# Sliding-window attention and a feed-forward layer on one core: part of the first batch's V is loaded in runs of five rows, TensorE puts the rows in order, and w_in is loaded after all of V

## The chip, the cores and the metric

The kernel runs on one core of one Trainium2 chip. A core has TensorE (PE, matrix products; weight loads into it are listed apart as PEld), VectorE (DVE), ScalarE (ACT), GpSimd (POOL) and SyncE (SP, which here only issues transfers), and 16 DMA engines that move data between the chip's memory and the core's SBUF. TensorE writes to PSUM; here DVE and ACT read PSUM. The metric is the device time of one execution in microseconds (us). Before the change it is 318.2 us, the median of three runs (317.32 to 319.56).

## The reference

```python
def _attn_ref(q, k, v):                 # (8, 8, 576, 64) each: batch, head, position, width
    scores = (1 / sqrt(D)) * q @ k.transpose(0, 1, 3, 2)
    mask = abs(pos[:, None] - pos[None, :]) <= 32
    scores = where(mask, scores, -1e9)
    attn = softmax(scores)
    return attn @ v

def _moe_ref(x, w_in, w_out, s, b):     # x: 4608 x 512, w_in: 512 x 2048, w_out: 2048 x 512
    r = maximum(x @ w_in, 0)
    return (s * r * r + b) @ w_out
```

The attention's heads are put side by side to make x. The input and output are float32; the kernel multiplies in bf16.

## The kernel before

All 8 batches go through in one stream. A batch has 576 positions, cut into 9 tiles of 64; two tiles make a **unit** of 128 keys, so batch 0 has units 0 to 3 and a last unit 4 of 64 keys. For batch 0 q and k are loaded in pairs of heads (`load_pair`, L583), cast to bf16 (L592, L593), turned by TensorE (L599), copied out of PSUM (L605, L606), multiplied to scores (L832) and put through exp (L854). V is loaded by unit (`load_v`, L566): 128 keys on the 128 partitions, and on each the 8 heads of that key, which lie far apart in memory, so that a row moved is 64 float32, 256 bytes. `cast_v` (L575) casts a unit to bf16 into the tile `vb`. For each unit TensorE multiplies the exponentials by `vb` (L747), where a column of ones in `vb` makes the softmax's sums; unit u needs V of units u and u-1. DVE takes the reciprocal of the sums (L769) and normalises (L771), TensorE turns the result (L778) and ACT copies it to `xt` (L786), the layer's input.

The feed-forward layer goes over blocks of positions: the first four blocks hold 96, 128, 128 and 160 positions. `s1` multiplies a block by w_in (L980), ACT takes the relu (L987) and DVE the square (L989) into `gt`; `s2` multiplies by w_out (L998). For the first four blocks `early` does it in small groups (L1029) as parts of w_out arrive. w_in comes in four quarters of two loads each (`load_weights`, L538), cast by POOL (L541); w_out likewise, into the same eight staging buffers `STG`, so a load of w_out waits until POOL has cast what was in its buffer.

The order of the work is not written by hand beyond the loads: every step is a task with an engine, a cost in ns, what it reads and writes, and a key. `_Graph.plan` goes through the tasks with these costs and fixes one order for each engine; `emit` adds the waits. On the chip each engine then does its tasks strictly in that order, so a task that waits holds all that stands behind it on its engine. The loads of the start have ordered keys (`nxt()`) and go out on one queue, SP's, in the order in which they are written: q and k in pairs, then `ORDER0`, then s and b, w_out, and the second batch's q, k and V.

Before the change `ORDER0` is units 0 and 1 of V, the first quarter of w_in (its number 8), units 2, 3 and 4 of V, and the other three quarters of w_in (9 to 11):

```python
ORDER0 = (0, 1, 8, 2, 3, 4, 9, 10, 11)
EV0 = ("pool", "dve", "pool", "dve", "pool")     # which engine casts each unit of V
```

Of the kernel before, what the change touches and what calls it, by code (L numbers as in the profile page):

```python
# [7 lines left out]
BF16 = mybir.dt.bfloat16  # L8
# [3 lines left out]
S = 576  # L12
D = 64
# [4 lines left out]
NPAIR = H // 2  # L18
NTILE = S // 64
NUNIT = (NTILE + 1) // 2  # L20
# [4 lines left out]
LAG = 1  # L25
K0 = ("dve", "dve", "dve", "dve")
Q0 = ("act", "pool", "pool", "pool")
ORDER0 = (0, 1, 8, 2, 3, 4, 9, 10, 11)
WINE = ("pool", "pool", "pool", "pool")
FIRST = ((0, 0), (1, 0), (2, 0), (0, 1), (1, 1), (2, 1), (3, 0), (3, 1), (0, 2), (1, 2), (2, 2), (3, 2), (0, 3), (1, 3), (2, 3), (3, 3))  # L30
WOUTE = (("pool", "pool"),) * 4
# [9 lines left out]
CASTE = (("pool", "pool"), ("pool", "dve"))  # L41
SLACK = (1000.0, 2000.0, 3000.0, 3000.0)
PACEV = ((-1,-1,0,0,1),(0,0,1,1,2),(0,0,1,1,2))
EV0 = ("pool", "dve", "pool", "dve", "pool")
BANK1 = ("W", "SC", "SC", "AVN", "AVN")
EV1 = ("pool", "pool", "pool", "pool", "pool")
EV2 = ("dve",) * 5
# [24 lines left out]
class _Graph:  # L72
# [13 lines left out]
    def add(self, stream, fns, cost, reads=(), writes=(), key=0.0, accum=False, dma=None, waits=(),  # L86
            lat=None, slack=0.0):
        if not isinstance(fns, list):
            fns = [fns]
        after = [self.chain] if key < -100 and self.chain else []  # L90
        t = _Task(len(self.tasks), stream, fns, cost, self.LAT[stream] if lat is None else lat, key,
                  dma, slack, after)
        t.deps.update(waits)
        for a in after:
            assert a.stream == stream
            a.next.append(t)
        for r in reads:
            assert r in self.writer, r
            t.deps.add(self.writer[r])
        for w in writes:  # L100
            if w in self.writer:
                t.deps.add(self.writer[w])
            if not accum:
                t.deps.update(self.readers.get(w, ()))
        t.deps.discard(t)
        for r in reads:
            self.readers.setdefault(r, []).append(t)
        for w in writes:
            self.writer[w] = t
            if not accum:  # L110
                self.readers[w] = []
        self.tasks.append(t)
        if key < -100:
            self.chain = t
        return t
# [201 lines left out]
def bass_sliding_window_symmetric__then__act_starrelu_kernel(  # L317
# [23 lines left out]
    with ExitStack() as es:  # L341
# [11 lines left out]
        def sb(shape, dt, nm):  # L353
            uid["n"] += 1
            return es.enter_context(nc.sbuf_tensor(f"{nm}_{uid['n']}", list(shape), dt))
# [31 lines left out]
        ONESW = sb((128, 128), BF16, "onesw")  # L387
        IDENT = sb((128, 128), BF16, "ident")
        GT = [sb((128, 16, 512), BF16, "gt") for _ in range(2)]
        R1 = [sb((128, 512), BF16, "r1") for _ in range(NR1)]  # L390
        OUTS = [sb((128, DM), F32, "outs") for _ in range(NOUT)]
        CVEC = sb((128, DM), F32, "cvec")
# [134 lines left out]
        def load_weights(which, i, x, key, eng):  # L527

            si = take("stg", NSTG)
            stg = STG[si].rearrange("p (a c) -> p a c", a=2)  # L530
            if which == "in":
                src = moe_w_in.rearrange("(kc p) f -> p kc f", p=128)[:, 2 * x:2 * x + 2, i * 512:(i + 1) * 512]
                dst = WIN_BF[:, 2 * x:2 * x + 2, i * 512:(i + 1) * 512]
            else:
                f0 = 4 * i + 2 * x
                src = moe_w_out.rearrange("(fc p) c -> p fc c", p=128)[:, f0:f0 + 2, :]
                dst = WOUT_BF[:, f0:f0 + 2, :]
            add("sp", lambda e: e.dma_start(stg, src), 600.0, writes=[("STG", si)], key=key,  # L538
                dma=("l", 16, 100.0 if which == "in" else 85.0))
            land[which, i, x] = g.tasks[-1]  # L540
            add(eng, (lambda e: e.copy(dst, stg)) if eng == "act" else (lambda e: e.tensor_copy(dst, stg)),  # L541
                {"act": 1040.0, "dve": 690.0, "pool": 1100.0}[eng], reads=[("STG", si)], writes=[("W" + which, i, x)],
                key=key + 150.0, slack=100.0)
# [12 lines left out]
        def load_v(c, u, key, eng, waits=()):  # L556

            vs = number(c, u) % NUNIT
            ts = tiles(c, u)
            at = [tile_at(c, t) for t in ts]  # L560
            if len(at) == 2 and at[0][0] == at[1][0]:
                at = [at[0] + (0, 128)]
            else:
                at = [x + (64 * i, 64) for i, x in enumerate(at)]
            n = sum(x[3] for x in at)
            add(eng, [lambda e, b=b, j=j, p0=p0, m=m: e.dma_start(  # L566
                VST[p0:p0 + m, vs, :, :], v[b, :, 64 * j:64 * j + m, :].rearrange("h p d -> p h d"))
                for b, j, p0, m in at],
                (650.0 if eng == "sp" else 500.0) * len(at), writes=[("VST", vs)], key=key, dma=("l", n // 2, (20.0, 17.0, 23.0)[min(c, 2)]), waits=waits)
            land["v", c, u] = g.tasks[-1]  # L570

        def cast_v(c, u, key, eng, slack):
            vs, vb, n = number(c, u) % NUNIT, number(c, u) % (2 * NUNIT), 64 * len(tiles(c, u))
            add(eng, (lambda e: e.copy(VB[0:n, vb, :, 0:D], VST[0:n, vs, :, :])) if eng == "act" else
                (lambda e: e.tensor_copy(VB[0:n, vb, :, 0:D], VST[0:n, vs, :, :])),  # L575
                {"act": 617.0, "dve": 420.0, "pool": 750.0}[eng],
                reads=[("VST", vs)], writes=[("V", vb)], key=key, slack=slack)

        def load_pair(b, name, pr, load_key):

# [310 lines left out]
        def attention():  # L891
            seq = {"k": -200.0}

            def nxt():
                seq["k"] += 1.0
                return seq["k"]

            def w(which, i):
                for x in (0, 1):
                    load_weights(which, i, x, nxt(), WINE[i] if which == "in" else WOUTE[i][x])  # L900

            for pr in range(NPAIR):
                for name in "qk":
                    load_pair(0, name, pr, nxt())
                    turn_pair(0, name, pr, -60.0 + 0.1 * pr, banks, K0[pr] if name == "k" else Q0[pr], 200.0)
                pair_scores(0, pr)
            for t in ORDER0:
                if t < 8:
                    load_v(0, t, nxt(), "sp")
                    cast_v(0, t, -28.0 + t, EV0[t], 300.0)  # L910
                else:
                    w("in", t - 8)
            first_units()
            masks(land["av", 0, NUNIT - 1])
            for i, src in enumerate((moe_s, moe_b)):
                add("sp", lambda e, i=i, src=src: e.dma_start(SROW[0:128:32, i:i + 1], src.partition_broadcast(4)),
                    600.0, writes=[("SROW", i)], dma=("l", 1, 15.0), key=nxt())
            add("dve", lambda e: e.stream_shuffle(SB128[:, :], SROW[:, :], [0] * 32), 150,
                reads=[("SROW", 0), ("SROW", 1)], writes=[("SB128", 0), ("SB128", 1)], key=P2[0] - 8.0, slack=500.0)
            for step in ORDER1:  # L920
                if step[0] == "w":
                    w("out", step[1])
                elif step[0] == "v":
                    load_v(1, step[1], nxt(), "sp")
                    cast_v(1, step[1], due(1, 0) - 4.0 + step[1], EV1[step[1]], 800.0)
                else:
                    for name in "qk":
                        load_pair(1, name, step[1], nxt())
            yield S
            for pr in range(NPAIR):  # L930
                for name in "qk":
                    turn_pair(1, name, pr, due(1, 0) - 4.0 + 0.1 * pr, banks, "dve" if name == "k" else "pool", 500.0)
                pair_scores(1, pr)
            for u in range(NUNIT):
                if u == NUNIT - 1:
                    pe_part(due(1, u) - 3.0, None, qk_part(1, u))
                    exp_mask(1, u, due(1, u) - 3.0)
                last.append((1, u))
                close()
                yield closed[0]  # L940
            for b in range(PAIRS, B):
                c = seq_of(b)
                later(b, due(c, group_of(b)[0]) - 24.0)
                for i, u in enumerate(group_of(b)):
                    load_v(c, u, due(c, u) - 35.0, late(b), [paced(b, PACEV[min(b, 4) - 2][i])])
                    cast_v(c, u, due(c, u) - 4.0, EV2[i], SLACK[3])
                for u in group_of(b):
                    unit(c, u)
                    yield closed[0]
            if seq_tiles(LONG) % 2 == 0:  # L950
                unit(LONG, seq_units(LONG) - 1)
            while last:
                close()
            yield T
# [373 lines left out]
```

## Time and profile before

| | |
|---|---|
| median of 3 runs | 318.2 us |
| the profiled execution | 316.0 us |
| its span, from the first instruction to the last | 314.2 us |
| busy in the span | PE 297.0, DVE 190.1, ACT 140.8, POOL 89.3 us |
| first matmul of attention times V (L747) | at 14.25 us |
| first matmul of the layer (L980) | at 17.33 us |
| casts of w_in by POOL | the first at 14.28 us, the last at 29.02 us |

Times in the profile count from the span's start. In a row of the timeline stand the start, the duration (of the whole run of like instructions), the engine, the line and operation, the tiles written and read, the tile or shape, the count, and in square brackets how long the engine had been idle and what released it. In the chain of waits, which is followed back from the last instruction, stand start, duration and what that time was; "issue" is time in which the engine waited for nothing that the profile shows. In the page's slices each digit is a fortieth of the span, in tenths. In a window's row stand the window, its length, the busy time of PE, PEld, DVE, ACT and POOL with the number of instructions, the clock granted to TensorE as a share of the full one, the mean busy share of the 16 DMA engines, and GB/s.

### The profile page before, as it was taken

What the parts mean: (1) busy time and instruction counts of PE and PEld (TensorE: products, weight loads), DVE (VectorE), ACT (ScalarE), POOL (GpSimd) and SP (SyncE); (2) the same over time, 40 slices, a digit from 0 to 9 for tenths busy, and PEclk for the clock granted to TensorE, in tenths of its full rate; (3) what the DMA queues carried; (4) which work ended last, traced back from release to release, by engine and by line L of the source; (5) the groups of instructions that cost most, each with busy time, mean ns of one, the idle gap of its engine ahead of it and who ended that gap; (6) DMA issues with size and microseconds to landing.
All of it is one profiled execution on the core that took longest, in us unless ns stands there. A gap on an engine that the chain in (4) does not pass through costs nothing.

```text
span 314.2 us, 8417 instructions
## 1 busy us (share of the span) xinstructions
PE 297.0 (95%) x3557; PEld 162.3 (52%) x3602; DVE 190.1 (61%) x377; ACT 140.8 (45%) x219; POOL 89.3 (28%) x109
## 2 busy tenths in 40 slices
PE   7698999899999999999999999999999999999995
PEld 3477855477644554544444444444444444444444
DVE  3455594875796796887578477856555543333312
ACT  4736435266635775653266335444444333333300
POOL 3468864635136136132313421260000000000000
PEclk9969999999999999999999999999999999999999
DMA  7999999998998998798999799997111110100122
GB/s 261 296 303 392 388 286 282 191 172 263 254 166 210 288 160 163 237 228 140 219 297 165 161 190 336 166 157 176 52 52 50 52 46 33 37 35 33 37 96 74
DMA packets 98985, 56.13 MB, mean 179 GB/s; under 512 B 74048, under 2 KB 88128, under 8 KB 98944
## 3 DMA queue, kind: packets, MB, share of 16 engines
q1 hardware_dynamic: 98944, 55.56, 74.8%
q8 instruction: 29, 0.48, 0.7%
q14 instruction: 12, 0.10, 0.1%
HBM read 36.70 MB, written 9.44 MB: 147 GB/s over the span
## 4 chain that ended last, share of the span: by engine, by line
PE 79%; DMA 9%; DVE 4%; issue 3%; POOL 2%; ACT 2%; SPq 1%; POOLq 0%
PE w L980 34%; PE o L998 32%; DMA stg<-in_k_dram 4%; PE avn L747 3%; DMA stg<-in_moe_w_in_dram 3%; DMA vst<-in_v_dram 2%; PE o L1029 2%; PE avn L1029 2%; DVE gt L989 2%; PE sc L689 2%; PE w L599 1%; ACT r L987 1%; PE avn L778 1%; POOL win L541 1%; DVE outs L1014 1%
## 5 line engine op out<-in xcount | busy, mean ns | idle before, releaser
L980 PE MATMUL w<-xt,win 128*128 128x512 bf16 (+4 forms) x813 | 141.3, 315 | 3.6 <-issue 1.9
L987 ACT ACTIVATE r<-w 128x512 bf16<-128x512 f32 (+2 forms) x148 | 86.6, 586 | 107.2 <-PE w L980 88.8
L998 PE MATMUL o<-wout,gt 128*128 128x512 bf16 (+1 forms) x510 | 123.1, 372 | 2.0 <-issue 1.4
L989 DVE TENSOR_TENSOR gt<-r 128x512 bf16<-128x512 bf16 (+2 forms) x148 | 75.0, 511 | 79.3 <-ACT r L987 78.7
L980 PEld LDWEIGHTS w<-xt,win 128*128 128x128 bf16 x832 | 70.2, 99 | 53.8 <-issue 0.8
L998 PEld LDWEIGHTS o<-wout,gt 128*128 128x128 bf16 x528 | 50.5, 98 | 54.6
L638 POOL CAST nat<-stg 128x1024 bf16<-128x1024 f32 (+1 forms) x21 | 24.6, 1174 | 62.1 <-DMA stg<-in_q_dram 41.3
L655 POOL COPY kt<-ktr 128x512 bf16<-128x512 bf16 (+1 forms) x30 | 30.8, 1027 | 38.4 <-DMA ktr<-nat 36.9
L717 ACT ACTIVATE ex<-sc 128x1024 bf16<-128x1024 f32 (+1 forms) x29 | 29.7, 1023 | 22.2 <-PE avn L747 21.3
L1014 DVE SCALAR_TENSOR_TENSOR outs<-o,sb,cvec 128x512 f32<-128x512 f32 (+1 forms) x35 | 25.4, 729 | 13.6 <-PE o L998 13.5
L721 DVE TENSOR_TENSOR ex<-ex,mask 128x1024 bf16<-128x1024 bf16 (+1 forms) x29 | 23.0, 794 | 1.6 <-ACT ex L717 0.6
L771 DVE TENSOR_TENSOR xn<-avn,rec 128x512 bf16<-128x512 f32 (+1 forms) x31 | 21.4, 690 | 0.9
L747 PE MATMUL avn<-vb,ex 64*64 64x65 bf16 x952 | 20.1, 199 | 0.6 <-issue 0.3
L747 PEld LDWEIGHTS avn<-vb,ex 64*64 64x64 bf16 x952 | 13.1, 108 | 13.8 <-issue 7.6
L638 DVE CAST nat<-stg 128x1024 bf16<-128x1024 f32 (+1 forms) x15 | 12.7, 849 | 2.3 <-DMA stg<-in_q_dram 1.3
L575 DVE CAST vb<-vst 128x512 bf16<-128x512 f32 (+1 forms) x30 | 13.0, 439 | 1.4 <-DMA vst<-in_v_dram 1.4
L689 PE MATMUL sc<-qt,kt 64*64 64x128 bf16 x440 | 11.7, 216 | 0.0
L769 DVE RECIPROCAL rec<-avn 128x8 f32<-128x8 f32 (+1 forms) x31 | 6.3, 203 | 6.9 <-PE avn L747 6.6
L786 ACT COPY xt<-avn 128x512 bf16<-128x512 bf16 (+2 forms) x14 | 7.2, 523 | 6.2 <-PE avn L778 6.2
L1029 PE MATMUL o<-wout,gt 128*128 128x512 bf16 x29 | 8.2, 379 | 1.0 <-POOL mask L508 0.8
L541 POOL CAST win<-stg 128x1024 bf16<-128x1024 f32 x8 | 8.4, 1048 | 1.8 <-DMA stg<-in_moe_w_in_dram 1.4
L1029 PE MATMUL avn<-wout,gt 128*128 128x512 bf16 x27 | 8.1, 380 | 0.7 <-issue 0.6
(90 smaller groups left out, 137.7 us busy)
## 6 DMA issues: line engine op xcount, KB each, us to landing
out_dram<-outs SPq DMA_DIRECT2D x35, 256.0 KB, 2.6
vst<-in_v_dram SPq DMA_DIRECT2D x32, 256.0 KB, 5.9
stg<-in_q_dram SPq DMA_DIRECT2D x6, 1024.0 KB, 6.8
stg<-in_k_dram SPq DMA_DIRECT2D x6, 1024.0 KB, 10.4
stg<-in_moe_w_in_dram SPq DMA_DIRECT2D x8, 512.0 KB, 6.4
stg<-in_moe_w_out_dram SPq DMA_DIRECT2D x8, 512.0 KB, 10.0
stg<-in_q_dram SPq DMA_DIRECT2D x8, 288.0 KB, 4.9
stg<-in_k_dram SPq DMA_DIRECT2D x8, 288.0 KB, 4.8
```

The source lines that it names most:

```text
L638: add(eng, lambda e, x=x: e.tensor_copy(nat[0:top, 1024 * x:1024 * x + 1024].rearrange("p (i h d) -> p h i d", h=H, i=2), stg[0:top, :].re ...
L655: add("pool", lambda e, c=c, w=w: e.tensor_copy(KT[slot][:, :, c:c + w].rearrange("p a (s i) -> p a s i", i=4), KTR[slot][:, :, :, c // 4: ...
L717: add("act", lambda e, dst=flat_dst, src=flat_src: e.activation(dst, src, AF.Exp, bias=0.0, scale=0.125), 190 + 0.833 * 512 * len(hs), rea ...
L721: add("dve", lambda e, flat=flat, mask=mask: e.tensor_tensor(flat, flat, mask, ALU.mult), 130 + 0.53 * 512 * len(hs), reads=[("E", ei, hp, ...
L747: return [lambda e: e.matmul(av[64 * x:64 * x + 64, h, 0:D + 1], lhsT=buf[64 * g:64 * g + 64, h % 2, h // 2, c:c + 64], rhs=VB[64 * g:64 * ...
L771: add("dve", lambda e: e.tensor_tensor(XN[xi][0:p1, :].rearrange("p (a c) -> p a c", a=H), av[0:p1, :, 0:D], REC[ri][0:p1, :].rearrange("p ...
L980: add("pe", [lambda e, g=g, kc=kc: e.matmul(wt[:, g, :], lhsT=WIN_BF[:, kc, (f0 + g) * 128:(f0 + g + 1) * 128], rhs=XT[:, kc, t0 % XR:t0 % ...
L987: add("act", lambda e: e.activation(rt, wt, AF.Relu, bias=0.0, scale=1.0), 190 + 0.833 * ng * nt, reads=[("W", wb)], writes=[("R1", rb)], ...
L989: add("dve", lambda e: e.tensor_tensor(GT[gs][:, f0:f0 + ng, g0:g0 + nt], rt, rt, ALU.mult), 130 + 0.53 * ng * nt, reads=[("R1", rb)], wri ...
L998: add("pe", [lambda e, fc=fc: e.matmul(O[:, ob, 0:cn], lhsT=GT[gs][:, fc, g0:g0 + 128], rhs=WOUT_BF[:, fc, c0:c0 + cn], start=(fc == 0), s ...
L1014: add("dve", lambda e: e.scalar_tensor_tensor(OUTS[us][:, 0:cn], bank, SB128[:, 0:1], CVEC[:, c0:c0 + cn], ALU.mult, ALU.add), 200 + 1.07 ...
L1029: add("pe", [lambda e, fc=fc, bank=bank, gs=gs, g0=g0: e.matmul(bank, lhsT=GT[gs][:, fc, g0:g0 + 128], rhs=WOUT_BF[:, fc, :], start=(fc == ...
```

## The change

Units 0 and 1 of V are loaded as before. Keys 256 to 575 (units 2 to 4) come in another way: `load_rows` loads two heads at a time. For each head the 320 keys are cut into 64 runs of five consecutive keys; one run of 5 x 64 float32 is 1,280 contiguous bytes and goes to one partition, the first head to partitions 0 to 63 and the second to 64 to 127. There are four such loads (two in each call), and two casts to bf16, by POOL and DVE, into `VN`, which lies in a buffer of `gt` that is not yet used.

The keys are now five to a partition. `pick` makes a matrix of zeros with ones, and `place_v` multiplies by it: ten matmuls of 256 columns for each unit (five for each half of the partitions) put every key on its own partition in a PSUM bank, and ACT or DVE copies the bank to `vb`. This is exact, since each result is one number times one.

w_in is loaded after all of V, its eight loads in a row. In the order that the planner gives, the ordering matmuls of unit 2 stand on TensorE between the products of units 0 and 1, those of unit 3 after the product of unit 1, and those of unit 4 before the turning of unit 1; the first matmuls of the layer stand after the products of units 2 and 3. On DVE the cast of the second half of the runs stands ahead of the reciprocal of unit 0. On POOL the cast of the first half stands ahead of all casts of w_in. The later order differs in places on all engines, with the same instructions. The planner's cost of a w_in load is changed from 100 to 86 ns a row.

```diff
-ORDER0 = (0, 1, 8, 2, 3, 4, 9, 10, 11)
+HEAD, RUN = 2, 5
+ORDER0 = (("v", 0), ("v", 1), ("r", 0), ("r", 1), ("w", 0), ("w", 1), ("w", 2), ("w", 3))
+ROWE = ("pool", "dve")
+BANK0 = ("W", "AVN", "W")
...
-EV0 = ("pool", "dve", "pool", "dve", "pool")
+EV0 = ("pool", "dve", "act", "dve", "act")
...
+        VN = GT[1][:, 0:3, :].rearrange("p x c -> p (x c)")[:, 0:NPAIR * RUN * D].rearrange("p (a i d) -> p a i d", a=NPAIR, i=RUN)
+        PICK = sb((128, 65, RUN), BF16, "pick")
...
-                dma=("l", 16, 100.0 if which == "in" else 85.0))
+                dma=("l", 16, 86.0 if which == "in" else 85.0))
...
+        def load_rows(y, load_key):
+
+            dst = VST[:, HEAD:NUNIT, :, :].rearrange("p u h d -> p (u h d)")[:, 0:NPAIR * RUN * D].rearrange(
+                "p (a c) -> p a c", a=NPAIR)
+            add("sp", [lambda e, pr=pr: e.dma_start(
+                dst[:, pr, :], v[0, 2 * pr:2 * pr + 2, 128 * HEAD:S, :].rearrange("h (p i) d -> h p (i d)", i=RUN))
+                for pr in (2 * y, 2 * y + 1)], 960.0, writes=[("VS", y)], key=load_key, dma=("l", 16, 56.0))
+            eng = ROWE[y]
+            add(eng, lambda e: e.tensor_copy(
+                VN[:, 2 * y:2 * y + 2, :, :].rearrange("p a i d -> p a (i d)"), dst[:, 2 * y:2 * y + 2, :]),
+                {"dve": 450.0, "pool": 780.0}[eng], reads=[("VS", y)], writes=[("VN", y)], key=-28.0 + y, slack=200.0)
+            land["rows", y] = g.tasks[-1]
+
+        def pick():
+
+            add("dve", lambda e: e.memset(PICK[:, :, :], 0.0), 150, writes=["PICK"], key=-57.0)
+            add("dve", [lambda e, p0=p0: e.tensor_copy(PICK[p0:p0 + 64, 0:64, RUN - 1], IDENT[p0:p0 + 64, p0:p0 + 64])
+                        for p0 in (0, 64)], 250, reads=["IDENT"], writes=["PICK"], key=-57.0)
+
+        def place_v(u, eng):
+
+            name = BANK0[u - HEAD]
+            bank, res, n = {"W": W, "AVN": AVN}[name], [(name, 0), (name, 1)], 64 * len(tiles(0, u))
+            c0 = RUN - 1 + 128 * (u - HEAD)
+            grid = PICK.rearrange("p a r -> p (a r)")
+            add("pe", [lambda e, i=i, hp=hp: e.matmul(
+                bank[0:n, hp, 0:256].rearrange("p (a c) -> p a c", a=NPAIR),
+                lhsT=grid[64 * hp:64 * hp + 64, c0 - i:c0 - i + n], rhs=VN[64 * hp:64 * hp + 64, :, i, :],
+                start=(i == 0), stop=(i == RUN - 1), skip_group_check=True) for i in range(RUN) for hp in (0, 1)],
+                650.0, reads=[("VN", 0), ("VN", 1), "PICK"], writes=res, key=-26.5 + u, slack=300.0)
+            dst = VB[0:n, u, :, 0:D].rearrange("p (a i) c -> p i a c", i=2)
+            src = bank[0:n, :, 0:256].rearrange("p i (a c) -> p i a c", a=NPAIR)
+            add(eng, (lambda e: e.copy(dst, src)) if eng == "act" else (lambda e: e.tensor_copy(dst, src)),
+                {"act": 620.0, "dve": 600.0}[eng], reads=res, writes=[("V", u)], key=-26.5 + u)
...
-            for t in ORDER0:
-                if t < 8:
+            pick()
+            for name, t in ORDER0:
+                if name == "v":
                     load_v(0, t, nxt(), "sp")
                     cast_v(0, t, -28.0 + t, EV0[t], 300.0)
+                elif name == "r":
+                    load_rows(t, nxt())
                 else:
-                    w("in", t - 8)
+                    w("in", t)
+            for u in range(HEAD, NUNIT):
+                place_v(u, EV0[u])
...
-                    load_v(1, step[1], nxt(), "sp")
+                    load_v(1, step[1], nxt(), "sp", [land["rows", y] for y in (0, 1)])
```

## The prediction

> **What bounds the kernel now.** I read the page's engine shares and slices first, then the chain of waits up to 32 us, then the timeline of TensorE there, then busy time by window for clock and DMA rate.
>
> ```profile
> span 314.2 us, 8417 instructions
> ...
> PE 297.0 (95%) x3557; PEld 162.3 (52%) x3602; DVE 190.1 (61%) x377; ACT 140.8 (45%) x219; POOL 89.3 (28%) x109
> ...
> PEclk9969999999999999999999999999999999999999
> DMA  7999999998998998798999799997111110100122
> ```
>
> TensorE is busy 95% of the span, so after the start whatever delays TensorE delays the end. The one slice with a low clock (6) and the full DMA queue (9) lie in the first 40 us: there TensorE waits for inputs, and there the whole change sits. The chain of waits says which:
>
> ```profile
> 10.24 6.61 DMA vst<-in_v_dram
> ...
> 16.98 0.63 POOL vb L575
> ...
> 18.54 8.66 DMA stg<-in_moe_w_in_dram
> 27.21 0.03 issue
> 27.23 0.02 POOLq L293
> 27.25 0.08 issue
> 27.33 1.05 POOL win L541
> ...
> 31.80 0.38 PE o L1029
> ```
>
> V and then w_in come off one SP queue in the order of issue; the end of each load sets the next step. TensorE in the same stretch:
>
> ```profile
> 14.25 0.74 PE L747 MATMUL sc<-vb,ex 64*64 64x65 bf16 x24 [0.47 <-ACT ex L854]
> 14.95 0.94 PE L747 MATMUL o<-vb,ex 64*64 64x65 bf16 x32
> 16.02 0.61 PE L778 MATMUL sc<-ident,xn 128*128 128x128 bf16 x4
> 16.93 0.61 PE L778 MATMUL o<-ident,xn 128*128 128x128 bf16 x4 [0.31 <-DVE xn L771]
> 17.33 1.49 PE L980 MATMUL w<-xt,win 128*128 128x96 bf16 x16
> 18.75 0.94 PE L747 MATMUL avn<-vb,ex 64*64 64x65 bf16 x32
> 19.50 0.93 PE L747 MATMUL sc<-vb,ex 64*64 64x65 bf16 x32
> 20.36 1.64 PE L980 MATMUL w<-xt,win 128*128 128x128 bf16 x16
> ```
>
> At 20.36 us units 0 to 3 have had their attention-times-V products and the first feed-forward group is done. I use this state as the mark against which the changed kernel is timed. From here to the end only two gaps of over 0.5 us belong to this stretch: 0.63 before 26.68 and 0.76 before 31.80, both behind weights.
>
> ```profile
> 16.00:19.00 3.00, 2.67 (x40) 2.27 (x40) 1.27 (x3) 1.21 (x3) 1.54 (x3) 0.50 1.02 212
> 22.00:40.00 18.00, 16.30 (x262) 14.19 (x262) 9.44 (x21) 10.27 (x21) 15.70 (x25) 1.00 1.05 390
> ```
>
> The last three columns are clock, DMA share and GB/s. V in 256-byte rows moves at 212 GB/s, weights in 2,048-byte rows at 390. The clock is half from 14.8 to 21.6 us, after TensorE was busy for only 0.66 of the 2 us from 12 to 14.
>
> **The new loads.** Per DMA engine (a sixteenth of the rate): 256 B take 19.3 ns, 2,048 B take 84 ns; on the straight line between them a 1,280-byte run takes 56 ns. Ends: 52 ns at the weights' rate, 97 ns at V's rate. Removed: units 2 to 4 of V, 320 keys x 8 heads = 2,560 rows, 160 on each of 16 engines, 3.1 us. Added: four loads of 128 runs. What they cost hangs on one thing that no row of before shows: over how many engines a load is dealt when its two sides have different shapes. The destination is 128 partitions; the source is 2 heads x 64 runs x 320 numbers, and it cannot be joined into 128, because the heads lie 36,864 numbers apart and 64 runs cover 20,480. Every large load of before has the same outermost count on both sides (128, 64 or 16). The ends:
> - 16 engines: 8 runs each, 0.45 us a load, 1.8 us in all, 1.3 us less than before.
> - 2 engines, one per head: 64 runs each, 3.6 us a load; the four stand behind each other on the same two engines, 14.4 us in all.
>
> The nearest row is the load of moe_s and of moe_b, the only ones with a small outermost count (4): the trace records 5 updates of their semaphore where every other load of that queue has 16. With four numbers to move it could hardly be otherwise, but it shows that the spread is not always 16 and goes with the outermost count. I take 2 engines.
>
> The Trainium skill (page "DMA: Bandwidth & Descriptors", section "Why a DMA increments its semaphore by 16 and not by 1") states that a copy runs on the largest number of engines, at most 16, that divides the slowest counts of both sides; by it 2 and 128 give 2, and the sum is the one of two engines. The same page's "Specifications" asks for rows of at least 512 B for full rate, which speaks for the change and would by itself give the 1.3 us.
>
> **When the rows are there.** The cast of V's unit 0 began on its landing at 11.13; unit 1 is 64 rows x 19.3 ns later, 12.3 us. The four loads follow: 12.3 + 14.4 = 26.7 us. The SP queue holds behind them too: before the change the issues of the first two w_in loads took 3.73 us from 6.47 with two V loads ahead, where a q or k load's takes 0.43; so the other 14 engines run dry. w_in's part on the two engines comes after: 16 rows x 84 ns = 1.35 us a load, first quarter at 29.4, and POOL's 1.05 us cast ends it at 30.5.
>
> **What waits for them.** The written order decides here. DVE has the cast of the second half (nearest row: 0.42 us for 512 columns, so 0.5 for 640) ahead of the reciprocals and normalisations of units 0 and 1, so those stand behind 26.7 as well. TensorE has the first ten ordering matmuls behind unit 0's product and ahead of unit 1's: everything from there on waits to 26.7 + 0.1 + 0.5 = 27.3 us. Nothing covers this; about 12 us of TensorE idle appear, and by the row above the clock is half again afterwards.
>
> An ordering group is 10 matmuls of 256 columns. Row of L1029 in the chain: two of 512 columns in 0.43 us, so 0.108 us for 256 at full clock. One by one 1.08 a group, two row halves side by side 0.54 (16 matmuls of L832 with 128 columns take 0.35 us, under half of one by one, so halves do run together). At half clock 1.1 to 2.2; I take 1.1, and 0.8 for the last group where the clock may be returning. The path: 27.3 + 1.1 (group) + 0.94 (unit 1) + 1.1 (group) + 0.6 (transposes) + 0.8 (group) + 0.4 (transposes) + 0.75 + 0.75 (units 2, 3, between 0.94 at half and 0.6 at full clock) = 33.7. The ScalarE and DVE copies out of PSUM (about 0.6 each, by the 0.59 of L786) fall beside these products. w_in is ready at 30.5, so it is not last. The first feed-forward group takes 0.9 at full clock (33 such matmuls took 1.80 at 24.24): the mark is reached at 34.6 instead of 20.4, **14.2 us later**.
>
> Given back: the two gaps, since weights are now ahead of TensorE (1.4 us), and half of the 1.2 us at half clock between 20.4 and 21.6 (0.6). Net +12.2. The DMA stream by itself says 14.4 - 3.1 = 11.3 later for w_out and the second batch, up to 2.4 less if the engine that lagged in before (by the semaphore updates the sixteen parts of each of the last two w_in loads landed over 2.4 us) is not one of the two: 8.9 to 11.3. TensorE's path is the longer one; the other is the floor. From 70 to 310 us TensorE is busy 234.5 of 240 us, so nothing later absorbs it.
>
> Hidden edits: the memset and two copies for the 0/1 matrix on DVE (0.1 to 0.3 us each) lie in the 2.3 us in which DVE waits for the first k load (2.1 to 4.4). POOL's half cast stands ahead of two memsets and the w_in casts, which wait for later loads anyway. The waits put on the second batch's V loads are long satisfied. The planner also writes the later order anew; I cost that at 0, within 1 us either way.
>
> **Sum.** The profiled execution took 316.0 us, 1.8 more than its span. 316.0 + 12.2 = 328.2. The median of the runs, 318.2, is 2.2 above that execution; I forecast the median: **330**.
>
> **Rivals.**
> 1. Sixteen engines, ending not slower. For: the line through the rows gives 1.8 us for the four loads. Then they land at 14.1, w_in's end comes 1.3 us earlier, but 3.2 us of ordering matmuls at half clock join TensorE's path; less idle before 21.6 can bring the clock back up to 3.4 us earlier, worth 1.7. -1.3 + 3.2 - 1.7 = +0.2: 318.4. Against: the source's outermost 2. It decides from 8 engines up: there the loads take 3.6 us, 0.5 more than before; at 4 they take 7.2, and the sum is still +5.
> 2. Sixteen engines, with the ordering not covered: no clock gain and no w_in gain, +3.2: 321.4.
> 3. Two engines and a cold clock all along, halves not side by side: each group 2.2, +3.6 on the path: 333.8. Runs at V's byte rate (97 ns) would add up to 10.
>
> **How the numbers follow.** Two engines 0.87 (rival 3 is 0.1 of it), rival 1 0.09, rival 2 0.04. Range: low end the DMA floor with 52 ns runs, 318.2 + 8.9 - 1.1 = 326, less 2 for the new order and for runs as quick as the profiled one: 324; high end rival 3 with runs some 20% dearer: 337. That leaves out rivals 1 and 2 and little else. A change within 1% (3.2 us) is about what a measurement of this kernel cannot tell from none. Faster 0.02 (rival 1 at its best), same 0.09, slower 0.89.
>
> **What would show it.** In the changed profile: the DMA share falls to about 2/16 between 13 and 26 us; the loads of the runs land some 3.6 us apart, the last near 27; DVE's reciprocal of unit 0 starts after 27 instead of 15.03; TensorE idles from about 15 to 27; the first feed-forward group starts near 34 instead of 17.33, and the clock row shows a second low slice. I am wrong if the four loads land within 2 us of each other near 14; then the time is rival 1's or 2's.

## The result, and the profile after

The changed kernel takes **329.1 us** (median of 5 runs, 328.17 to 332.64), beside 318.2 us (317.32 to 319.56) for the kernel before on the same chip: a ratio of 1.037, with a 95% interval of 1.030 to 1.043. It is 10.9 us slower. Its profiled execution took 330.8 us, 1.7 above its median, where that of before lay 2.2 below its own; the two profiles differ by 14.8 us, the medians by 10.9. A few executions of some kernels ran in a slower state; ratios are of the others alone, and so are the medians and clocks from here on.

The page of the changed kernel, its total, the busy times, and the slices of TensorE, clock and DMA:

```profile
span 329.1 us, 8511 instructions
...
PE 305.3 (93%) x3632; PEld 163.6 (50%) x3632; DVE 194.2 (59%) x381; ACT 141.7 (43%) x221; POOL 93.4 (28%) x108
...
PE   8607799998999999998899999999999999999996
...
PEclk9956999999999999999999999999999999999999
DMA  7479989997799599999899979998511111100012
```

The third digit of TensorE is 0, the clock has two low slices (5 and 6) where it had one, and the DMA row has a 4 in its second slice, where it was 9. The chain of waits of the changed kernel (start, duration, what) names the load:

```profile
9.72 1.64 SPq L588
11.37 0.04 issue
11.41 14.65 DMA vst<-in_v_dram
26.06 0.02 issue
26.08 0.51 DVE gt L592
26.59 0.05 issue
26.63 1.25 PE w L609 x9
...
32.73 1.68 PE w L1025 x32
```

The chain goes from the fourth load of runs, 14.65 us after its issue, through DVE's cast of the second half to the first ordering group. Stretches of 2 us of the changed kernel; the last three columns are clock, DMA share and GB/s:

```profile
12.00:14.00 2.00, 1.39 (x56) 0.89 (x54) 1.32 (x3) 1.31 (x2) 0.00 (x0) 1.00 0.13 49
14.00:16.00 2.00, 0.71 (x30) 0.41 (x24) 0.00 (x0) 1.98 (x4) 0.00 (x0) 1.00 0.17 58
16.00:18.00 2.00, 0.00 (x0) 0.00 (x0) 0.00 (x0) 0.10 (x1) 0.20 (x1) 0.73 0.13 49
18.00:20.00 2.00, 0.00 (x0) 0.00 (x0) 0.00 (x0) 0.00 (x0) 1.14 (x3) 0.50 0.63 186
20.00:22.00 2.00, 0.00 (x0) 0.00 (x0) 0.00 (x0) 0.00 (x0) 0.00 (x0) 0.50 1.04 337
```

0.13 is 2/16: two of the sixteen DMA engines work, and they move 24.5 GB/s each, so a run of 1,280 B takes 52 ns. From about 18.5 us on the other fourteen are busy again, with w_in. TensorE and DVE in the same stretch, from their timelines:

```profile
14.56 0.71 PE L787 MATMUL sc<-vb,ex 64*64 64x65 bf16 x24 [0.48 <-ACT ex L894]
26.63 1.25 PE L609 MATMUL w<-gt,pick 64*128 64x256 bf16 x10 [11.37 <-DVE gt L592]
27.81 0.94 PE L787 MATMUL o<-vb,ex 64*64 64x65 bf16 x32
28.69 1.25 PE L609 MATMUL avn<-gt,pick 64*128 64x256 bf16 x10
29.87 0.61 PE L818 MATMUL sc<-ident,xn 128*128 128x128 bf16 x4
30.41 0.79 PE L609 MATMUL w<-gt,pick 64*64 64x256 bf16 x10
...
32.66 1.75 PE L1025 MATMUL w<-xt,win 128*128 128x96 bf16 x32
```

```profile
26.08 0.49 DVE L592 CAST gt<-vst 128x640 bf16<-128x640 f32 x1 [12.19 <-DMA vst<-in_v_dram]
26.49 0.20 DVE L809 RECIPROCAL rec<-sc 128x8 f32<-128x8 f32 x1
```

TensorE stands still for 11.4 us, and the reciprocal of unit 0, whose product ended at 15.27, stands behind the cast. The layer's first matmul moves from 17.33 to 32.66 us. POOL's casts of w_in move less, the last of the eight from 29.02 to 37.41:

```profile
17.80 0.72 POOL L592 CAST gt<-vst 128x640 bf16<-128x640 f32 x1 [5.94 <-DMA vst<-in_v_dram]
...
27.30 1.04 POOL L546 CAST win<-stg 128x1024 bf16<-128x1024 f32 x1 [8.04 <-DMA stg<-in_moe_w_in_dram]
...
37.41 1.04 POOL L546 CAST win<-stg 128x1024 bf16<-128x1024 f32 x1
```

So 10.9 us of loss lie between two shifts: 15.3 us for TensorE's first layer matmul and 8.4 us for the last of w_in. Which of them the end follows is a question of its own below.

### The profile page after: what moved, and what is told of

Same layout as the page of the kernel before. It is cut to its first block, busy times and chain, and to the rows that moved or that the text cites. A ratio compares the mean times of both kernels' runs of the same rounds, so it can differ in the third digit from the quotient of the medians.

```text
span 329.1 us, 8511 instructions
## 1 busy us (share of the span) xinstructions
PE 305.3 (93%) x3632; PEld 163.6 (50%) x3632; DVE 194.2 (59%) x381; ACT 141.7 (43%) x221; POOL 93.4 (28%) x108
## 4 chain that ended last, share of the span: by engine, by line
PE 79%; DMA 9%; DVE 5%; SPq 3%; issue 2%; ACT 1%; ACTq 0%
PE w L1025 33%; PE o L1043 32%; DMA vst<-in_v_dram 6%; PE avn L787 4%; DVE gt L1034 3%; DMA stg<-in_k_dram 3%; PE avn L1074 2%; PE sc L729 2%; PE o L1074 1%; SPq L588 1%; ACT r L1032 1%; SPq L623 1%; PE w L639 1%; PE avn L818 1%; SPq L571 1%
## 5 line engine op out<-in xcount | busy, mean ns | idle before, releaser
L1025 PE MATMUL w<-xt,win 128*128 128x512 bf16 (+4 forms) x832 | 143.8, 314 | 2.0 <-issue 1.3
L1043 PE MATMUL o<-wout,gt 128*128 128x512 bf16 (+1 forms) x528 | 126.5, 373 | 0.0
L1034 DVE TENSOR_TENSOR gt<-r 128x512 bf16<-128x512 bf16 (+2 forms) x148 | 76.5, 524 | 73.4 <-ACT r L1032 73.3
L1025 PEld LDWEIGHTS w<-xt,win 128*128 128x128 bf16 x832 | 68.9, 98 | 54.7 <-issue 1.4
L678 POOL CAST nat<-stg 128x1024 bf16<-128x1024 f32 (+1 forms) x21 | 27.8, 1324 | 60.6 <-DMA stg<-in_q_dram 35.8
L695 POOL COPY kt<-ktr 128x512 bf16<-128x512 bf16 (+1 forms) x30 | 32.3, 1077 | 38.5 <-DMA ktr<-nat 37.0
L678 DVE CAST nat<-stg 128x1024 bf16<-128x1024 f32 (+1 forms) x15 | 12.7, 846 | 6.8 <-DMA stg<-in_k_dram 4.0
L609 PE MATMUL w<-gt,pick 64*128 64x256 bf16 (+1 forms) x20 | 2.0, 349 | 11.4 <-DVE gt L592 11.4
L1074 PE MATMUL avn<-wout,gt 128*128 128x512 bf16 x32 | 8.9, 381 | 0.2 <-DVE gt L1034 0.2
## 6 DMA issues: line engine op xcount, KB each, us to landing
stg<-in_k_dram SPq DMA_DIRECT2D x6, 1024.0 KB, 10.9
```

The source lines that it names most:

```text
L678: add(eng, lambda e, x=x: e.tensor_copy(nat[0:top, 1024 * x:1024 * x + 1024].rearrange("p (i h d) -> p h i d", h=H, i=2), stg[0:top, :].re ...
L695: add("pool", lambda e, c=c, w=w: e.tensor_copy(KT[slot][:, :, c:c + w].rearrange("p a (s i) -> p a s i", i=4), KTR[slot][:, :, :, c // 4: ...
L1025: add("pe", [lambda e, g=g, kc=kc: e.matmul(wt[:, g, :], lhsT=WIN_BF[:, kc, (f0 + g) * 128:(f0 + g + 1) * 128], rhs=XT[:, kc, t0 % XR:t0 % ...
L1034: add("dve", lambda e: e.tensor_tensor(GT[gs][:, f0:f0 + ng, g0:g0 + nt], rt, rt, ALU.mult), 130 + 0.53 * ng * nt, reads=[("R1", rb)], wri ...
L1043: add("pe", [lambda e, fc=fc: e.matmul(O[:, ob, 0:cn], lhsT=GT[gs][:, fc, g0:g0 + 128], rhs=WOUT_BF[:, fc, c0:c0 + cn], start=(fc == 0), s ...
L1074: add("pe", [lambda e, fc=fc, bank=bank, gs=gs, g0=g0: e.matmul(bank, lhsT=GT[gs][:, fc, g0:g0 + 128], rhs=WOUT_BF[:, fc, :], start=(fc == ...
```

## The experiments

**Theory:** the loss is the dealing of the four loads over two DMA engines, because the source's outermost count is 2. **Rivals:** w_in standing behind all of V costs the time; the 30 ordering matmuls cost it; or SP's issue does. Ratios are to the kernel before on the same chip (its median was 318.1 or 318.2 in all three comparisons). Starts and landings are read from the one profiled execution of each kernel, whose own time can lie some us off the median; the table at the end has both.

### One head a load, outermost count 64

```diff
-            add("sp", [lambda e, pr=pr: e.dma_start(
-                dst[:, pr, :], v[0, 2 * pr:2 * pr + 2, 128 * HEAD:S, :].rearrange("h (p i) d -> h p (i d)", i=RUN))
-                for pr in (2 * y, 2 * y + 1)], ...
+            add("sp", [lambda e, pr=pr, hp=hp: e.dma_start(
+                dst[64 * hp:64 * hp + 64, pr, :], v[0, 2 * pr + hp, 128 * HEAD:S, :].rearrange("(p i) d -> p (i d)", i=RUN))
+                for pr in (2 * y, 2 * y + 1) for hp in (0, 1)], ...
```

> Eight loads of one head each (64 partitions, 64 runs of 1,280 bytes) in place of four of two heads; same bytes, same tiles, same order on TensorE, DVE, ACT and POOL. Theory (a load is dealt over as many engines as its source's outermost count allows, 2 before, 16 now): the runs take about 1.8 us on the queue, the cast of the second half on DVE starts near 15 instead of 26.08, TensorE's idle of 11.4 us goes, time 318.4, between 316 and 321. Rival (the ordering matmuls and the new order on the engines cost it): the time stays over 326, since none of them changes.

Measured: 321.8 us, ratio 1.011 (1.005 to 1.017). 7.3 of the 10.9 us are gone, and nothing but the shape and the number of the loads was changed. But the time is not that of before. SP's timeline of this kernel:

```profile
7.29 9.08 SPq L588 DMA_DIRECT2D vst<-in_v_dram  x8
16.41 3.57 SPq L543 DMA_DIRECT2D stg<-in_moe_w_in_dram  x6
```

SP needs 9.08 us for the eight issues; the ones in which it doesn't wait take 0.60 each. The DMA share is 0.26 to 0.50 from 12 to 18 us and the last run lands at 18.2. By these rows SP's issue had become the limit, which no expectation had; a later study tests it.

### Four heads a load, outermost count 4

Runs of ten keys, so that two neighbouring pairs of heads make one load; the keys come out of the ordering in another order.

```diff
+            add("sp", [lambda e: e.dma_start(
+                dst[:, 2 * y:2 * y + 2, :].rearrange("p a c -> p (a c)"),
+                v[0, 4 * y:4 * y + 4, 128 * HEAD:S, :].rearrange("h (p i) d -> h p (i d)", i=2 * RUN))], ...
```

> Two loads of four heads each, 32 runs of ten keys (2,560 bytes) a head, so the source's outermost count is 4; the keys land in another order than the 0/1 matrix puts right, so V's last 320 keys of the first batch are mixed up; sizes and order of all other work are unchanged. Theory: 4 engines, 32 runs of about 105 ns each, 3.4 us a load and 6.7 together: DVE's cast starts near 19.2, DMA share near 4/16 in that stretch, time near 322, between 320 and 325. Rival (the transfer of many heads at once is slow for another reason, say its distance in memory): the end of the loads does not move with the outermost count and stays near 26, time near 329.

Measured: 324.7 us, ratio 1.018 (1.012 to 1.025). The dose answers: outermost 2, 4 and 64 give +10.9, +6.6 and +3.7 us (the last with eight issues of SP). The ordering starts at 23.05, later than expected:

```profile
23.05 1.25 PE L609 MATMUL w<-gt,pick 64*128 64x256 bf16 x10 [7.43 <-DVE gt L592]
```

A load took its four engines 5.2 us, 164 ns for 2,560 bytes, where the rate of two engines alone (24.5 GB/s each) would give 105. The w_in loads were under way beside it (DMA share 1.0 to 1.1); that this slowed it was not tested apart.

### One head a load, with the first quarter of w_in ahead of the runs

```diff
-ORDER0 = (("v", 0), ("v", 1), ("r", 0), ("r", 1), ("w", 0), ("w", 1), ("w", 2), ("w", 3))
+ORDER0 = (("v", 0), ("v", 1), ("w", 0), ("r", 0), ("r", 1), ("w", 1), ("w", 2), ("w", 3))
```

> As the run with one head a load, but the first quarter of w_in goes ahead of the runs, as it goes ahead of unit 2 in the kernel before. Theory: the runs land about 2.7 us later (near 16.8) and the first feed-forward group can start earlier; both wait for the ordering matmuls, 317 to 320. If the place of w_in behind V costs by itself, this is faster than the run with one head a load by over 1 us.

Measured: 321.3 us, ratio 1.009 (1.005 to 1.013), the same as without this edit within the intervals. The place of that quarter doesn't matter.

### The order alone, in the kernel before

```diff
-ORDER0 = (0, 1, 8, 2, 3, 4, 9, 10, 11)
+ORDER0 = (0, 1, 2, 3, 4, 8, 9, 10, 11)
```

> The kernel before with only the order of the loads changed: all five units of V in 256-byte rows, then the eight loads of w_in. Theory: V's last unit lands near 15.5, the first quarter of w_in near 18.2 and its cast ends near 19.3, so the first feed-forward group starts some 2 us later than 17.33 while the attention products move ahead of it; 317.5 to 320, no clear change. Rival (w_in behind V is what costs): over 322.

Measured: 318.5 us, ratio 0.999 (0.996 to 1.003). The time is the same: the rival of w_in's place falls. In the profiled execution the layer's first matmul starts at 21.84 instead of 17.33; that execution took 320.2 us, so it doesn't show that the lateness was free.

### Two heads a load, but outermost count 64

Four loads of two heads, as in the change; each goes to one half of the partitions, with runs outermost and heads inside.

```diff
+            add("sp", [lambda e, hp=hp: e.dma_start(
+                dst[64 * hp:64 * hp + 64, 2 * y:2 * y + 2, :],
+                v[0, 4 * y + hp:4 * y + hp + 3:2, 128 * HEAD:S, :].rearrange("h (p i) d -> p h (i d)", i=RUN))
+                for hp in (0, 1)], ...
```

> Four loads for the runs as in the changed kernel, two heads each, but each load goes to one half of the partitions and its source is turned so that the outermost count is 64 on both sides: 64 runs x 2 heads. Nothing else is changed. In the study with one head a load, all 16 engines took part, yet the last run landed only at 18.2 us, and SP issued the eight loads at 0.60 us each. Theory A (what was left there is SP's issue, a fixed time for a load): four issues save about 2.4 us, the last run lands near 15, TensorE starts the ordering at 15.5 to 16.3 instead of 18.75, and the time is 318.3 to 320. Theory B (the issue goes with the number of runs, 0.6 us for 64): nothing is gained, 321 to 322.5, the ordering starts near 18.7. If the spread over engines were not set by the outermost count, it would fall back to some 329.

Measured: **318.3 us, ratio 1.001 (0.998 to 1.004)**. The same runs, bytes, number of loads, order and matmuls as in the change, and the whole loss is gone. SP issues a load of 128 runs in 0.60 to 0.61 us, as it did one of 64: a fixed time for a load, which is theory A. So the two engines were the whole loss, and the 3.5 us that eight loads still cost were the price of that remedy: four more issues of SP. TensorE in this kernel:

```profile
17.32 1.25 PE L610 MATMUL w<-gt,pick 64*128 64x256 bf16 x10 [0.70 <-DVE gt L593]
...
24.11 1.75 PE L1026 MATMUL w<-xt,win 128*128 128x96 bf16 x32
```

The layer starts 6.8 us later here than in the kernel before (17.33). But this execution took 321.5 us, the longest of the 13, 3.2 above their median; at what time the layer starts in the others is not on record.

### The same with two of each ten ordering matmuls

```diff
-                start=(i == 0), stop=(i == RUN - 1), skip_group_check=True) for i in range(RUN) for hp in (0, 1)],
+                start=True, stop=True, skip_group_check=True) for i in range(1) for hp in (0, 1)],
```

> The loads of the study with two heads and 64 outermost, and of each group of ten ordering matmuls only the first two are left (the others, and so the right order of keys 256 to 575, are left out). If the ordering is on the path at its full price (three groups of 1.25 us), 8/10 of it goes: 3.0 us less than with all matmuls, by 2.0 to 3.3 after what the colder clock takes back. If it was covered by w_in, which lands at the same time, under 1 us less.

Measured: 318.7 us, ratio 1.003 (1.000 to 1.006): with 24 of 30 ordering matmuls left out nothing is gained. The number is that of the second branch; the reason it gave was w_in, and another can be argued. From 16 to 24 us, with all matmuls and then with two of ten:

```profile
16.00:24.00 8.00, 6.97 (x158) 4.21 (x149) 3.30 (x8) 3.54 (x6) 4.95 (x7) 0.57 1.00 351
```

```profile
16.00:24.00 8.00, 6.94 (x140) 5.07 (x138) 4.96 (x11) 3.32 (x6) 4.59 (x6) 0.50 0.96 325
```

The clock stays at half throughout without them. Over all runs the mean granted clock is 0.993 with all matmuls and 0.984 with two of ten; 0.9% of 317 us is 2.8 us at full clock, as much as the matmuls saved (3 groups x 0.85 = 2.6). So the ordering matmuls may pay for themselves by bringing the clock back. That is argued from equal sums and not shown: with all matmuls, the eight executions with a clock of 0.994 or 0.995 have a median of 318.3 us, and so have the five with 0.988 or 0.989; and in the profiled executions the 46th of the layer's 148 relus starts earlier with two of ten (111.97 us) than with all (113.88, and 113.26 in a second look). That w_in covers the ordering isn't excluded.

### Four heads a load, outermost count 64

```diff
+            if y == 0:
+                add("sp", [lambda e, hp=hp: e.dma_start(
+                    dst[64 * hp:64 * hp + 64, :, :],
+                    v[0, hp:hp + 7:2, 128 * HEAD:S, :].rearrange("h (p i) d -> p h (i d)", i=RUN))
+                    for hp in (0, 1)], ...
...
-                ... reads=[("VS", y)], ...
+                ... reads=[("VS", 0), ("VS", 1)], ...
```

> Two loads for the runs instead of four, four heads each, 64 runs x 4 heads, outermost 64 on both sides; both casts wait for both loads. Theory A (fixed time for a load at SP): 1.2 us less of SP than with four loads; but the transfer, some 1.8 us after V's own, becomes last: the rows land at 14.1 to 15, and the time is 0 to 1 us below that of four loads. Theory B (issue goes with the number of runs): as with four and eight loads, 321 to 322.5.

Measured: 318.1 us, ratio 1.001 (0.998 to 1.004), as four loads. In the profiled execution the rows landed later than expected, the last at 17.5 us and not at 15, and the last cast of w_in starts at 29.20; that execution took 322.3 us, the longest of the 13, so it says little of the median.

### Late weights alone, in the kernel before

```diff
-ORDER0 = (0, 1, 8, 2, 3, 4, 9, 10, 11)
+ORDER0 = (0, 1, 8, 2, 3, 4, 20, 9, 10, 11)
...
+                if t == 20:
+                    add("sp", [lambda e, hp=hp: e.dma_start(
+                        BALLAST[64 * hp:64 * hp + 61, 0, :], v[0, hp, 0:305, :].rearrange("(p i) d -> p (i d)", i=5))
+                        for hp in (0, 1)], ...
```

> The kernel before, V in its old rows, with two loads put between V and the second quarter of w_in; their data goes to a buffer of its own and is used by nobody. Each has 61 partitions on both sides; 61 has no divisor up to 16 but 1, so by the theory of the outermost count each of the two loads goes to a single DMA engine: 61 runs x 56 ns = 3.4 us, 6.8 us in all on one engine. If so, V, the first quarter of w_in and the mark stay where they were, and the last w_in load comes 4.5 to 7 us later than before (29.0 for the start of its cast). If the end follows the weights, the time is 4 to 8 us above before: 322 to 326. If the mark (first feed-forward group) is what decides, it is within 1 us of before. If 61 were dealt over 16 engines in some other way, the weights are under 1 us late and nothing is learned of the end.

Measured: 322.8 us, ratio 1.015 (1.012 to 1.019). Each of the two loads had one landing, at 21.08 and 24.32 us: 61 runs in 3.24 us, 53 ns a run, one engine, one load behind the other. TensorE of this kernel:

```profile
17.21 1.49 PE L985 MATMUL w<-xt,win 128*128 128x96 bf16 x16
...
28.29 7.80 PE L985 MATMUL w<-xt,win 128*128 128x96 bf16 x128 [3.24 <-POOL win L542]
```

The layer's start stays (17.21), the last cast of w_in starts 5.0 us later (34.02), and the time is 4.6 us longer, in the profiled execution 5.0 (321.0 against 316.0). Late weights alone are enough for a loss of this size.

### The ordering three times over

```diff
-                start=(i == 0), ... for i in range(RUN) for hp in (0, 1)],
+                start=(i == 0), ... for _ in range(3) for i in range(RUN) for hp in (0, 1)],
```

> The study with four loads of outermost 64, and each ordering group done three times over into the same bank (30 matmuls in place of 10, the last pass counts). Weights come as before; TensorE's first feed-forward group starts some 7.5 us later than the 24.1 with one pass (2.5 us more for each of three groups at half clock, less if the clock returns), near 31, which is close to the 32.7 of the changed kernel. If the end follows TensorE's mark, the time is 6 to 8 us above that study's 318.3: 324 to 326. If the end follows the weights and TensorE has that much slack, within 1 us of it. In between, TensorE's idle of some 2.5 us between 25 and 36 us is used up first: 321 to 324.

Measured: 320.8 us, ratio 1.009 (1.006 to 1.011), 2.5 above the study with one pass and in none of the three brackets. The delay that it was built for didn't come. The clock was at half from 16.1 to 19.6 us, and with one pass from 16.2 to 23.0, so it came back within the first group:

```profile
16.42 3.32 PE L610 MATMUL w<-gt,pick 64*128 64x256 bf16 x30 [1.05 <-DVE gt L593]
...
20.32 1.81 PE L610 MATMUL avn<-gt,pick 64*128 64x256 bf16 x30
...
25.68 1.75 PE L1026 MATMUL w<-xt,win 128*128 128x96 bf16 x32
```

60 matmuls more delay the layer's start by 1.6 us (24.11 to 25.68), and the last cast of w_in starts at 30.43, 1.05 later. They cost 2.5 us in the median. The study can't tell TensorE's delay from the weights'.

### A second look at four loads with outermost 64

> The study with four loads of outermost 64 once more, for a second profile: its first was of its slowest execution (321.5 against a median of 318.3), so it can't show how a mark that is 4.6 us late ends in no loss. If the loss is taken up by idle time of TensorE, an execution near the median has TensorE busy with no gap over 0.5 us from its first feed-forward group to 36 us, where the first profile had gaps of 1.86 and 0.40. If it is not, the gaps are there again and the gain lies later.

Measured: 321.0 us in its one execution, 2.6 above that kernel's median on another chip, where the kernel before took 315.4 in its one execution beside it. There was one gap over 0.5 us (0.90) in the stretch.

```profile
23.13 1.75 PE L1026 MATMUL w<-xt,win 128*128 128x96 bf16 x32
```

```profile
28.75 1.04 POOL L546 CAST win<-stg 128x1024 bf16<-128x1024 f32 x1
```

The layer starts 5.8 us later than in the kernel before, the last cast of w_in 0.3 earlier (28.75 against 29.02). So in this execution TensorE was late and the weights were not, and it was 5 us or more longer than the profiled ones of the kernel before (316.0 and 315.4). Neither branch is shown. Both profiles of this kernel are of executions slower than its median, and why they are is open; what the median execution does there can't be read from them.

The runs side by side. The first four columns are of the profiled execution, with its time in the fourth; the median and the mean granted clock are over the runs. The third column is the start of the 46th of the 148 relus that ACT does for the layer in each kernel, a mark well behind the start:

| kernel | first layer matmul | last w_in cast | 46th relu | this execution | median | clock |
|---|---|---|---|---|---|---|
| before | 17.33 | 29.02 | 109.63 | 316.0 | 318.2 | 0.987 |
| two heads, outermost 64, second look | 23.13 | 28.75 | 113.26 | 321.0 | | 0.989 |
| four heads, outermost 64 | 24.45 | 29.20 | 114.69 | 322.3 | 318.1 | 0.989 |
| two heads, outermost 64 | 24.11 | 29.38 | 113.88 | 321.5 | 318.3 | 0.993 |
| two heads, 2 of 10 matmuls | 21.66 | 29.71 | 111.97 | 318.5 | 318.7 | 0.984 |
| order alone | 21.84 | 30.31 | 113.79 | 320.2 | 318.5 | 0.983 |
| ordering three times | 25.68 | 30.43 | 113.27 | 319.4 | 320.8 | 0.993 |
| one head, quarter first | 24.64 | 30.91 | 114.97 | 322.7 | 321.3 | 0.986 |
| one head a load | 25.26 | 32.28 | 115.44 | 321.7 | 321.8 | 0.989 |
| late weights alone | 17.21 | 34.02 | 115.61 | 321.0 | 322.8 | 0.983 |
| outermost 4 | 29.70 | 34.45 | 118.65 | 326.6 | 324.7 | 0.979 |
| the change, outermost 2 | 32.66 | 37.41 | 122.28 | 330.8 | 329.1 | 0.975 |

Down the table the median rises with the column of w_in's end, but for 0.1 and 0.2 us in two places, and not with that of the layer's start. That puts starts beside medians of other executions, though. Within the profiled executions the reading is another: where w_in's end stays within 0.7 us of the kernel before (the four rows below it), the 46th relu comes 2.3, 3.6, 4.3 and 5.1 us late, and it does so in the order of the layer's starts, 21.66, 23.13, 24.11 and 24.45. These four do the relus in the same sequence as the changed kernel; in the kernel before, the order alone, the quarter first and the late weights the sequence differs, which can shift the 46th by about 1 us. The profiled execution of the kernel before is 2.2 us below its median, so against a median one the four may be less late; their order among each other doesn't hang on it.

## Why the prediction was right, and where it was not

The forecast was 330 (324 to 337), the time 329.1. Its cause, the two engines, is shown: with them +10.9 us, with the same loads turned to outermost 64 nothing in the median. How the lateness of the start reaches the end is shown only in part.

**Two engines.** Right. The trace has two landings for each load of runs; with outermost 4 there are four, with 64 sixteen, with 61 one. The Trainium skill's page "DMA: Bandwidth & Descriptors", section "Why a DMA increments its semaphore by 16 and not by 1", which takes the largest number up to 16 that divides the slowest counts of both sides, gives 2, 4, 16 and 1 and agrees with all four. The row that I had for it, moe_s and moe_b with 5 updates, is now understood: a load on fewer than 16 engines leaves one record about its issue and one for each engine, so 5 means four.

**When the rows are there.** The loads landed at 14.4, 17.7, 21.6 and 26.06 us; predicted was 3.6 apart and 26.7 for the last. A run took 52 ns (the low end that I had named) while the two engines worked alone, and 60 to 70 ns in the last two loads, after SP had let the other fourteen go on.

**The other fourteen engines.** Predicted as dry until the runs had landed, near 26.7, they were dry only until about 18.5. SP was held through the four issues (until 14.63), then issued w_in while the runs were still queued on the two engines. So w_in's first cast began at 27.3, not after 29.4. By the rows it made no difference to TensorE's first layer matmul, since TensorE was at the ordering and the products until 32.66.

**What waits.** Right in order and nearly in size. TensorE began at 26.63 (27.3). The groups took 1.25, 1.25 and 0.79 us (1.1, 1.1, 0.8). From the first of them to the layer's first matmul it was 6.0 us (6.4). The mark came near 33.5, +13.2 (34.6, +14.2).

**Given back, and the floor.** The prediction took TensorE's path to the mark as what the end follows, less 2.0, and the DMA stream as a floor of 8.9 to 11.3 below it. The pair of profiled executions bears the path out. The 46th relu, before and after:

```profile
109.63 0.60 ACT L987 ACTIVATE r<-w 128x512 bf16<-128x512 f32 x1 [0.27 <-PE w L980]
```

```profile
122.28 0.60 ACT L1032 ACTIVATE r<-w 128x512 bf16<-128x512 f32 x1 [0.27 <-PE w L1025]
```

It is 12.7 us late (the sequence differs between the two, which can shift this by about 1 us), where the net forecast was 12.2. So little of the mark's 13.2 was given back, some 0.5 and not 2.0, and the last cast of w_in, 8.4 late and below the floor, doesn't reach 12.7. The other 2.1 of the 14.8 between the two executions arose further on, where the prediction had nothing.

The medians say something else. They differ by 10.9, so that 2.3 of 13.2 would be given back; and the loads turned to outermost 64 cost nothing in the median, though TensorE's mark was 4.6 us late in the one profiled execution (24.11 + 0.87 = 25.0 against 20.4) and 3.6 late in the other. Both of those executions took 2.6 us or more above that median, so no execution of that kernel is on record whose start was late and that lost nothing. With the layer's start in its place and the weights 5.0 us later the loss was 4.6: weights can set the end too. Which of the two the end follows in a median execution of the changed kernel, where both are late, stays open. The 2.0 given back fits the 2.3 of that mixed sum and not the 0.5 of the pair, so that part of the agreement may be luck.

**Rival 1 and its terms.** Sixteen engines were forecast at 318.4; with them it takes 318.3. The clock did come back earlier: 0.993 against 0.987 in the mean of all runs is up to 1.9 us, predicted 1.7; that it bought this time is not shown. The weights' 1.3 us earlier did not come in the two profiled executions (last cast 29.38 and 28.75 against 29.02); in the first the DMA share fell to 0.77 between 14 and 16 us, where before it was 1.17. The ordering's 3.2 us don't show in the median: leaving out most of it gave back no time there, with a lower clock. At four engines I had +5; it is +6.6. Rival 2 (321.4) has the time of one head a load (321.8), but not its reason: that was SP's issues. Rival 3 adds up to 334.0 (330.4 + 3.6), not 333.8, and nothing hangs on it.

**Hidden edits and the new later order,** costed at nothing within 1 us, are all in the kernel that takes 318.3, and the zero holds in the median. The 2.2 us from profiled execution to median held for before; the changed kernel's profiled execution lay on the other side.

## What to carry to other kernels

Before a load's runs are made longer, write down the outermost count of its two sides: two heads of 64 runs into 128 partitions went to two DMA engines and cost 10.9 us, while the same bytes with 64 outermost cost nothing in the median. A few more loads to mend that are not free either, where one queue issues them all at 0.60 us each. And don't put the start of one execution beside the median of others: in such a table a TensorE start 6 to 7 us late looked free, while within the profiled executions themselves the layer was still 3.6 to 5.1 us behind that of the kernel before at the 46th relu. A mark behind the start, read in the same execution, says what a late start cost.

## What the runs showed that was not expected

- SP issued a load of runs in 0.60 us, whether it had 64 or 128 runs, where one of q or k with 128 rows took 0.43.
- 61 partitions put a whole load on one DMA engine: 3.24 us for 61 runs of 1,280 bytes.
- Leaving out 24 ordering matmuls saved no time (318.7 against 318.3), with the mean granted clock down from 0.993 to 0.984.
- Runs of 2,560 bytes on four engines took 164 ns each beside w_in's traffic; the rate of an engine working alone gives 105.
